# Four row loads may leave on ScalarE's queue, and the written-out order of a fused retention and mixer kernel is replaced

## The chip, the core and the metric

The kernel runs on one core of a Trainium2 chip. A core has five engines with instruction streams of their own: PE (TensorE, matrix products), DVE (VectorE), ACT (ScalarE), POOL (GpSimd) and SP (SyncE, which here only issues transfers). [...] Transfers are started from three places: SP's queue, ACT's queue (both "hardware" queues) and POOL's ("software"), and all are carried by the same 16 DMA engines. The metric is the device time of one execution in microseconds; lower is better.

## The reference: what is computed

A retention recurrence (eight heads, a fixed decay for each) over 768 steps is followed by an MLP mixer, for four batches:

```python
state = gamma[None, :, None, None] * state + np.einsum('bhd,bhe->bhde', k[:, :, t], v[:, :, t])
y[:, :, t] = scale * np.einsum('bhd,bhde->bhe', q[:, :, t], state)
...
x = np.ascontiguousarray(attn_out.transpose(0, 2, 1, 3)).reshape(B, S, H * D)
...
h = np.maximum(xt @ w_tok1, 0.0) @ w_tok2
u = x + h.transpose(0, 2, 1)
h2 = np.maximum(u @ w_ch1, 0.0) @ w_ch2
return (u + h2).astype(np.float32)
```

q, k and v are [4, 8, 768, 64]; the output is [4, 768, 512]; everything outside the chip is 32-bit.

## The kernel before

**Tiles.** 768 steps are six chunks of 128. The work of a batch falls into a *front* and a *back*. A front is done for each of four pairs of heads: k and q are scaled by powers of the decay (lines 343 and 345, tiles k16 and q16), turned so that the head dimension lies on partitions (kT, qT), multiplied into scores (453), masked on DVE (463, tile am) and multiplied with v (474). What comes from earlier chunks goes through the running state U (408 to 420), is scaled into block-diagonal tiles (434, 436) and multiplied with qT (483). The sum is cast to x16 (489), goes through the token mixer (503 with weights wt1, relu at 512 or 514, 523 with weights wt2), and is cast to u16 (529), copied to X (539) and turned into uT. A back takes uT of all four pairs through the channel mixer: the widening product (606 in batches 0 and 1; a seven-product scheme at 679 in batches 2 and 3), relu, and the narrowing product in the same seven-product manner (784, 810, 820, 830, 837), whose sums are added into X and written out (862, 746 to 761 for the last rows).

**Turning.** It is done in one of three ways, by a table: on PE with a copy behind it (377, 379, 568), or, in batches 2 and 3 throughout and for most uT of batch 1, by a transposing DMA on SP's queue (367, 553).

**Loads.** Rows of batches 0 and 1 and all weights come through POOL's queue (lines 257, 292, 295), which casts to 16 bit on the way. The first k comes on SP's. Rows of batches 2 and 3 (the table PLAIN) are loaded as they are, 384 KB each, by SP's queue at line 282; engines cast them afterwards (343, 345; v at 358 and 360). All of them share four buffers called row.

**Order.** The function builds a list of operations. Each has one way or several (which engine may do it, with a planner's cost in ns), operations that it needs, and buffers that it takes. No planner runs when the kernel is built: the string PLAN names each operation in the order of the program, the digit of its way where there is more than one, and the PSUM bank where it takes one. "+" and a digit puts that many *fillers* there, products of a zero tile at line 935 whose result nobody reads. placed() reads the string and the operations are emitted in that order, each to its engine's stream. An engine does its own instructions strictly in that order.

## Time and profile before

| | |
|---|---|
| three runs | 188.79, 189.35, 189.88 us; median 189.35 |
| the profiled execution | 189.72 us, of which 187.9 us are the profile's span |
| busy share of the span | PE 97%, DVE 87%, ACT 67%, POOL 19% |
| fillers | 62 products, 14.8 us busy |
| granted TensorE clock | 0.999 |
| chain that ended last | PE 82%, DMA 5%, ACT 5%, DVE 4% |

In rows of the timeline the columns are start, duration (both in us), engine, line, operation, tiles, and a count; the bracket holds the idle time before and what ended it. "SPq", "ACTq" and "POOLq" are the sequencers that issue transfers. In windows each row is a stretch, with the busy time of every engine in it, the granted clock, the mean share of the DMA engines and GB/s. In the groups the two numbers behind the bar are the total busy us and the mean ns of one instruction.

### The profile page before, as it was taken

What the parts mean: (1) busy time and instruction counts of PE and PEld (TensorE: products, weight loads), DVE (VectorE), ACT (ScalarE), POOL (GpSimd) and SP (SyncE); (2) the same over time, 40 slices, a digit from 0 to 9 for tenths busy, and PEclk for the clock granted to TensorE, in tenths of its full rate; (3) what the DMA queues carried; (4) which work ended last, traced back from release to release, by engine and by line L of the source; (5) the groups of instructions that cost most, each with busy time, mean ns of one, the idle gap of its engine ahead of it and who ended that gap; (6) DMA issues with size and microseconds to landing.
All of it is one profiled execution on the core that took longest, in us unless ns stands there. A gap on an engine that the chain in (4) does not pass through costs nothing.

```text
span 187.9 us, 5270 instructions
## 1 busy us (share of the span) xinstructions
PE 182.2 (97%) x2102; PEld 137.5 (73%) x2102; DVE 163.0 (87%) x424; ACT 126.2 (67%) x288; POOL 36.2 (19%) x45
## 2 busy tenths in 40 slices
PE   7999999999999999999999999999999999999993
PEld 3556789667679879767677988875589986656882
DVE  3789899978799998989896999999999988879973
ACT  7227789677868697579868696899975535682220
POOL 8992659520020001000103100210000000000000
PEclk9999999999999999999999999999999999999999
DMA  6999999999999799999999999998206464500133
GB/s 101 168 165 196 175 178 187 172 187 207 187 211 221 153 116 222 193 203 205 194 244 161 220 149 221 349 161 214 42 0 108 147 65 176 197 0 5 56 140 140
DMA packets 94233, 30.23 MB, mean 161 GB/s; under 512 B 84352, under 2 KB 91264, under 8 KB 94208
## 3 DMA queue, kind: packets, MB, share of 16 engines
q1 hardware_dynamic: 62560, 18.95, 56.1%
q0 software_dynamic: 30208, 8.46, 44.0%
q10 hardware_dynamic: 1440, 2.49, 4.5%
q8 instruction: 16, 0.26, 0.6%
q14 instruction: 9, 0.07, 0.2%
HBM read 26.74 MB, written 6.29 MB: 176 GB/s over the span
## 4 chain that ended last, share of the span: by engine, by line
PE 82%; DMA 5%; ACT 5%; DVE 4%; issue 1%; DVEq 0%; ACTq 0%
PE bank L606 14%; PE bank L820 13%; PE bank L679 12%; PE bank L830 9%; PE bank L935 6%; PE bank L523 6%; PE bank L503 6%; PE bank L453 3%; PE bank L474 3%; DMA qT<-q 3%; PE bank L746 3%; DMA uT<-u 2%; PE bank L483 2%; PE bank L408 2%; PE bank L377 2%; ACT h L622 2%
## 5 line engine op out<-in xcount | busy, mean ns | idle before, releaser
L463 DVE TENSOR_TENSOR am<-bank,mask 128x384 f16<-128x384 f32 x64 | 33.6, 549 | 4.4 <-PE bank L453 4.0
L606 PE MATMUL bank<-uT,wc 128*128 128x384 f16 x192 | 36.0, 326 | 0.0
L622 ACT ACTIVATE h<-bank 128x384 f16<-128x384 f32 x48 | 21.6, 491 | 9.1 <-PE bank L606 7.2
L606 PEld LDWEIGHTS <-wc 128*128 128x128 f16 x192 | 17.4, 98 | 9.1 <-DVE uT L575 0.2
L360 POOL CAST v<-row 128x768 f16<-128x768 f32 x7 | 7.4, 1067 | 76.6 <-DMA row<-in_v_dram 50.4
L696 DVE TENSOR_TENSOR h<-bank,us 128x384 f16<-128x384 f32 x36 | 18.9, 552 | 2.8 <-PE bank L679 1.8
L810 ACT COPY us<-bank 128x256 f32<-128x256 f32 x27 | 10.1, 377 | 15.8 <-PE bank L820 15.6
L820 PEld LDWEIGHTS <-hs 128*128 128x128 f16 x198 | 18.7, 98 | 2.4
L837 DVE TENSOR_TENSOR X<-X,bank 128x256 f32<-128x256 f32 x44 | 17.7, 414 | 2.4 <-PE bank L830 1.5
L691 ACT COPY us<-bank 128x384 f32<-128x384 f32 x36 | 16.3, 490 | 4.3 <-PE bank L679 3.3
L489 ACT CAST x<-bank 128x384 f16<-128x384 f32 x30 | 14.0, 487 | 6.7 <-PE bank L483 6.6
L420 DVE SCALAR_TENSOR_TENSOR U<-U,gp,bank 128x64 f32<-128x64 f32 x64 | 17.4, 275 | 1.0
L820 PE MATMUL bank<-wsum,hs 128*128 128x256 f16 x132 | 17.6, 273 | 0.0
L935 PE MATMUL bank<-zero 128*128 128x384 f16 x62 | 14.8, 382 | 1.1 <-DVE zero L928 1.1
L679 PE MATMUL bank<-hs,wsum 128*128 128x384 f16 x72 | 15.0, 326 | 0.1
L529 ACT CAST u<-bank 128x384 f16<-128x384 f32 x27 | 12.6, 487 | 3.5 <-PE bank L523 3.3
L523 PE MATMUL bank<-h,wt 128*128 128x128 f16 x192 | 14.8, 219 | 0.0
L434 ACT ACTIVATE diag<-U,gp 64x320 f16<-64x320 f32 x25 | 13.8, 558 | 0.4
L679 PEld LDWEIGHTS <-wsum 128*128 128x128 f16 x96 | 9.3, 97 | 6.4 <-issue 0.5
L503 PE MATMUL bank<-x,wt 128*128 128x128 f16 x192 | 13.7, 219 | 0.0
L830 PEld LDWEIGHTS <-h 128*128 128x128 f16 x132 | 12.5, 98 | 1.5
L539 ACT COPY X<-bank 128x384 f32<-128x384 f32 x28 | 13.4, 494 | 0.1
(89 smaller groups left out, 365.8 us busy)
## 6 DMA issues: line engine op xcount, KB each, us to landing
out_dram<-X SPq DMA_DIRECT2D x14, 256.0 KB, 4.3
row<-in_v_dram SPq DMA_DIRECT2D x8, 384.0 KB, 5.5
row<-in_k_dram SPq DMA_DIRECT2D x8, 384.0 KB, 6.0
row<-in_q_dram SPq DMA_DIRECT2D x8, 384.0 KB, 5.5
wc<-in_moe_w_ch_dram POOLq DMA_DIRECT2D x5, 512.0 KB, 12.6
out_dram<-X ACTq DMA_DIRECT2D x9, 256.0 KB, 3.0
row<-in_q_dram POOLq DMA_DIRECT2D x8, 192.0 KB, 6.1
v<-in_v_dram POOLq DMA_DIRECT2D x8, 192.0 KB, 8.4
```

Source lines behind the costliest of these rows:

```text
L420: nc.vector.scalar_tensor_tensor(out=u[:, c], in0=u[:, c - 1], scalar=gp[:, p:p + 1], in1=st, op0=ALU.mult, op1=ALU.add)
L463: nc.vector.tensor_tensor(am, SC[g].tile[:, :m * P].rearrange("p (i t) -> p i t", t=P), mask.to_broadcast([P, m, P]), ALU.mult)
L503: nc.tensor.matmul(acc[:, jt * P:(jt + 1) * P], wt1[:, i, jt * P:(jt + 1) * P], X16.tile[:, i], start=(i + jt == 0), stop=(i == NC - 1), s ...
L523: nc.tensor.matmul(Y[hf].tile[:, i * P:(i + 1) * P], wt2[:, jt, t], H1.tile[:, jt], start=False, stop=(jt == NJ - 1), skip_group_check=True)
L606: nc.tensor.matmul(acc[:, :SH], wc1[:, ct, ft * P:(ft + 1) * P], UT.tile[:, ct, sh * SH:(sh + 1) * SH], start=(ct == 0), stop=(ct == NP - 1))
L622: nc.scalar.activation(H2.tile[:, ft], A.tile[:, :SH], AF.Relu)
L679: nc.tensor.matmul(acc[:, :SH], left(ct), r[:, ct], start=first and ct == 0, stop=ct == 1, skip_group_check=True)
L696: nc.vector.tensor_tensor(into(hf)[:, ft], bank.tile[:, :SH], kept(j), ALU.add)
L820: nc.tensor.matmul(acc_[:, lo], l[:, j], r[:, j], start=first and j == 0, stop=j == K2 - 1, skip_group_check=True)
L830: nc.tensor.matmul(acc_[:, lo], l[:, j], r[:, j], start=first and j == 0, stop=j == K2 - 1, skip_group_check=True)
L837: (nc.vector if e == "DVE" else nc.gpsimd).tensor_tensor(dst(), dst(), b_(), ALU.add)
L935: nc.tensor.matmul(spare[:, :384], zero[:, :P], zero, start=True, stop=True)
```

## The change

Three things are edited. A plain row load has two ways now, SP's queue or ACT's. The load of k into the second half of a q tile no longer names the load of that q as a dependency in the planner's list. And PLAN is another string. The third decides everything about the order; the other two only say what the string may choose from.

```diff
 PLAN = (
-    "0b04000a0903010d05020c060f1h11i107+h1j00e1W11k0081X0h+41l01m0g+81w011v230k1z+21n41A2x50i1y1o1p0j1S01T11q1r0m"
...
+    "04000b050901030f0d0a060e021h1081i107+i1j01n11l21o1p1q1m1k11r1W31S01T1+81w021A1z1U41v560c2x20h1s1t01u00g1x+11Y1"
...
+        def emit_plain(e):
+            t = tile_of(s, [P, 2, NC, D], FP)
+            (nc.sync if e == "SP" else nc.scalar).dma_start(out=t, in_=src.rearrange("h (c p) d -> p h c d", p=P))
+
         def emit():
-            if plain:
-                t = tile_of(s, [P, 2, NC, D], FP)
-                nc.sync.dma_start(out=t, in_=src.rearrange("h (c p) d -> p h c d", p=P))
-                return
...
-            o = Op(ops, (-20, 0, b, p), [("SP", 500, 500, emit)], [], [s], dma=dma, behind=rows[-1] if rows else None)
+            o = Op(ops, (-20, 0, b, p), either(emit_plain, SP=(500, 500), ACT=(450, 450)) if plain else
+                   [("SP", 500, 500, emit)], [], [s], dma=dma, behind=rows[-1] if rows else None)
...
-            o = Op(ops, (-20, 0, b, p), [("POOL", 1000, 1000, emit)], [loads[b, p, "q"][2]], [], [s], dma=dma,
+            o = Op(ops, (-20, 0, b, p), [("POOL", 1000, 1000, emit)], [], [], [s], dma=dma,
```

Line numbers behind the edit are one higher in the changed kernel (935 becomes 936).

The new string holds 34 fillers where the old one held 62: 18 ahead of the first real product (17 before), and 16 between the real products of the first batch (45 before). 4 of the 24 plain row loads go by ACT's queue. Of the eight casts of a plain v to 16 bit five stand on POOL, two on DVE and one on ACT; before it was seven on POOL and one on ACT.

The first place is the head of POOL's stream, where the loads of batch 0 are issued. v, row and wt1, wt2 are the tiles that they fill. Before:

```order
L295 DMA v_122<-in_v_dram 128x12x64
L295 DMA row_90<-in_k_dram 128x12x64
L295 DMA v_179<-in_v_dram 128x12x64
L295 DMA row_116<-in_k_dram 128x12x64
L292 DMA row_225<-in_q_dram 128x2x384
L295 DMA v_257<-in_v_dram 128x12x64
L257 DMA wt1_78<-in_moe_w_tok1_dram 128x6x256
L257 DMA wt2_79<-in_moe_w_tok2_dram 128x2x768
```

Three loads of q stand ahead of these rows. In the changed kernel the whole head of the stream is:

```order
L295 DMA v_110<-in_v_dram 128x12x64
L292 DMA row_112<-in_q_dram 128x2x384
L292 DMA row_114<-in_q_dram 128x2x384
L295 DMA row_114<-in_k_dram 128x12x64
L292 DMA row_245<-in_q_dram 128x2x384
L295 DMA v_260<-in_v_dram 128x12x64
L295 DMA row_245<-in_k_dram 128x12x64
L292 DMA row_289<-in_q_dram 128x2x384
L295 DMA row_289<-in_k_dram 128x12x64
L295 DMA v_329<-in_v_dram 128x12x64
L257 DMA wt1_78<-in_moe_w_tok1_dram 128x6x256
L257 DMA wt2_79<-in_moe_w_tok2_dram 128x2x768
```

The first v has moved to the front, and one more load, the k of the last pair, now stands ahead of the two weights: ten loads in place of nine.

The second place is SP's stream where the turned tiles of batch 2's first pair are made: kT and qT are what its scores read, uT there is batch 1's. Before:

```order
L282 DMA row_1275<-in_k_dram 128x12x64
L367 DMA_TRANSPOSE kT_1375<-k16_1347 128x6x128
L282 DMA row_1411<-in_q_dram 128x12x64
L553 DMA_TRANSPOSE uT_1126<-u16_1314 128x6x128
L367 DMA_TRANSPOSE qT_1449<-q16_1373 128x6x128
L282 DMA row_1471<-in_v_dram 128x12x64
L282 DMA row_1515<-in_v_dram 128x12x64
L553 DMA_TRANSPOSE uT_1126<-u16_1446 128x6x128
```

In the changed kernel:

```order
L281 DMA row_1240<-in_k_dram 128x12x64
L554 DMA_TRANSPOSE uT_1254<-u16_1078 128x6x128
L281 DMA row_1333<-in_q_dram 128x12x64
L368 DMA_TRANSPOSE kT_1343<-k16_1322 128x6x128
L281 DMA row_1430<-in_v_dram 128x12x64
L368 DMA_TRANSPOSE qT_1487<-q16_1345 128x6x128
L281 DMA row_1510<-in_q_dram 128x12x64
L554 DMA_TRANSPOSE uT_1254<-u16_1268 128x6x128
L554 DMA_TRANSPOSE uT_1254<-u16_1404 128x6x128
```

The uT that stood between kT and qT now stands behind qT, and a load of v stands in its place.

The third place is ACT's stream a little earlier, where three of the four loads have come. h2 is the relu of batch 0's widening product, x16, k16, h1 belong to fronts of batches 1 and 2:

```order
L623 ACTIVATE h2_825<-bank6_1125 128x384
L281 DMA row_1159<-in_v_dram 128x12x64
L623 ACTIVATE h2_876<-bank4_1054 128x384
L490 CAST x16_1174<-bank7_1128 128x384
L623 ACTIVATE h2_825<-bank1_1162 128x384
L490 CAST x16_1174<-bank2_1151 128x384
L281 DMA row_1184<-in_k_dram 128x12x64
L344 ACTIVATE k16_1186<-row_901,gk_69 128x6x64
L513 ACTIVATE h1_1215<-bank1_1191 128x256
L623 ACTIVATE h2_876<-bank4_1181 128x384
L281 DMA row_1238<-in_q_dram 128x12x64
L623 ACTIVATE h2_876<-bank6_1217 128x384
```

Three or four other instructions stand between one load and the next; before, no load stood in ACT's stream at all.

More of the change, by code (lines that the diff above doesn't have):

```diff
@@ new lines @@
+    "7915n6h6ecj26l17a05P05QcK6f6B5Tce46i6cx6C16j5R05U06mck5W5cncI1c35S07c06k05X16n0cMcC6D1cf0J06o56pcN6A11dco0S0"
+    "7d0cQ46Edq7cR6q06rd25drcZ25V0cS7f46F36G0P06s06Hdsd06t0d86d16I6J6K6L01a7g1e7h7i7j7k1f6M1d577bdz0d9cT2da6udAdO3"
+    "6v0dPd3d66w1dQdBd7d4dh47I07K2dicU6N70367l16O6Q6R6Pdb10R0cVdcdC2dn7dd7m0dDdodEdpdj7J17e6x6V66W6S06T7n21356U16X0"
+    "7p0W07P4dk77qcL7Qdldmde1dfdgcW37R7r6Y77M18S06Z0V0dw17N0dF50U0cX7L1g7ocp700dGdHcYdx7OdR2dU71c7S7TbUdS71721e00T0"
+    "74dL37UdV8T0dy8m0e2dX1dYdt4e65dW750dTdM7V18n1760e10X0eb6dudZdNe7e3731cgec7X35127Ze477Ydv7v48i1dI0dJ0Y0cP17W0"
@@ L70 @@
+    "j0iw5iOixiyiziPicj16iA0iBiQj3j54jY5iCj2iDiJifiIiSiR6iGj4iTj6iXj7ke7iUiViEiHkfjbiYjcj8j9jejdhk0k62jZk7k0iFiejC"
+    "f31k1iWjajDk2jfjG4jEiKjgjijk6jH0jFjLk3jI3jN0jl0jM0jJk4k50jOjhjr1jPjRjQ0hG1jsjpjSjq0jTjUjvjKjVjW0jtjm4ju0jjjwjy"
+    "k8jxk9kajnjX1kbkgjA1jokhjzkijB1kckd0kjkkkl0"
 )
```

48 lines of the change are left out of this document (20 added, 28 removed).

## The prediction

> **What bounds the kernel now.** I read the page's totals first, then the busy time by stretches of 10 us, then the waits of PE.
>
> ```profile
> span 187.9 us, 5270 instructions
> PE 182.2 (97%) x2102; PEld 137.5 (73%) x2102; DVE 163.0 (87%) x424; ACT 126.2 (67%) x288; POOL 36.2 (19%) x45
> ...
> PE 82%; DMA 5%; ACT 5%; DVE 4%; issue 1%; DVEq 0%; ACTq 0%
> ...
> L935 PE MATMUL bank<-zero 128*128 128x384 f16 x62 | 14.8, 382 | 1.1 <-DVE zero L928 1.1
> ```
>
> PE is busy 97% of the span and carries 82% of the chain that ended last. But 62 of its products are fillers, so a busy PE is not yet a working PE. Where they stand decides.
>
> ```profile
> 1.13 5.62 PE L935 MATMUL bank<-zero 128*128 128x384 f16 x17 [1.13 <-DVE zero L928]
> ...
> 22.24 0.34 PE L935 MATMUL bank<-zero 128*128 128x384 f16 x1
> 22.42 0.83 PE L523 MATMUL bank<-h,wt 128*128 128x128 f16 x12
> ```
>
> All of them lie in the first 22.6 us (the first row and the last of them). Behind that PE hardly ever stops:
>
> ```profile
> PE bank L453 <- DMA qT<-q: 0.6, 1, 0.6
> PE bank L679 <- DMA uT<-u: 0.2, 1, 0.2
> PE bank L408 <- ACT h L622: 0.2, 1, 0.2
> ```
>
> So there are two regimes. Up to 22.4 us the first batch's data set the pace and fillers pass the time. From there on PE's own products do, with 1.0 us of named waits in 162 us. An order can win in the first regime what its data allow, and in the second about 1 us; it can lose more than that wherever it makes PE wait.
>
> **Fillers and the start.** The change takes 29 fillers out from between the real products and puts one more ahead of them. A late group of 9 in the chain of waits
>
> ```profile
> 15.12 1.57 PE bank L935 x9
> ```
>
> is 174 ns each, so 29 are worth 5.1 us if nothing stands behind them. I don't count on that, because something does: the token mixer's weights.
>
> ```profile
> 5.89 1.02 POOL L295 DMA_DIRECT2D v<-in_v_dram  x1
> 6.89 1.03 POOL L295 DMA_DIRECT2D row<-in_k_dram  x1
> ...
> 9.60 1.56 POOL L257 DMA_DIRECT2D wt<-in_moe_w_tok_dram  x2
> ```
>
> The issues by window give from issue to landing:
>
> ```profile
> v<-in_v_dram POOLq DMA_DIRECT2D x1, 192.0 KB, 6.9
> row<-in_k_dram POOLq DMA_DIRECT2D x1, 192.0 KB, 7.0
> wt<-in_moe_w_tok_dram POOLq DMA_DIRECT2D x1, 384.0 KB, 8.2
> wt<-in_moe_w_tok_dram POOLq DMA_DIRECT2D x1, 384.0 KB, 9.7
> ```
>
> The v of 5.89 lands at 12.8, the k of 6.89 at 13.9: this queue hands over a load of k every 1.1 us, and later loads lag more and more behind their issue. wt1, issued at 9.6, lands at 17.8 and wt2, issued at 10.4, at 20.1. In the new order one more k goes ahead of it, so wt2 lands at 21.2, and line 523 can't run earlier. Its relu comes to DVE behind a row of mask products; I take 21.6, against 22.42 now: 0.8 us. Two small corrections nearly cancel. The new order has one more turn of k and two more products of line 483 ahead of that point (6 and 2 products, 0.45 us at the 56 ns that 12 products of line 523 take each in 0.67 us), which is work won. Against it, it moves both x16 casts of the second pair from ACT to DVE, with a mask product between them:
>
> ```profile
> L489 DVE CAST x<-bank 128x384 f16<-128x384 f32 x2 | 1.1, 544 | 0.0
> L463 DVE TENSOR_TENSOR am<-bank,mask 128x384 f16<-128x384 f32 x64 | 33.6, 549 | 4.4 <-PE bank L453 4.0
> 23.09 0.83 PE L503 MATMUL bank<-x,wt 128*128 128x128 f16 x12
> ```
>
> Three of these are 1.6 us behind the relu, while PE has 12 products of line 523 and half of line 503 to do, 1.0 us: it waits 0.6. The term is **-0.7 us**. Its bounds: DVE works 22.0 of the 25 us from 7 to 32 us (the sum over five windows, below) and has much the same rows to do, so its 3.0 us of idle are all that any order can win here; and if the weights' delay of 1.1 us simply passes through, the start is 1.1 us slower.
>
> ```profile
> sum 25.00, PE 24.84 PEld 18.61 DVE 22.02 ACT 16.32 POOL 17.74; mean PE 4.97 PEld 3.72 DVE 4.40 ACT 3.26 POOL 3.55
> ```
>
> **Batch 2's first turned q.** PE's longest wait:
>
> ```profile
> 61.17 1.14 ACT L343 ACTIVATE q<-row,gy 128x384 f16<-128x384 f32 x2
> ...
> 63.23 1.96 SPq L553 DMA_TRANSPOSE uT<-u  x1
> 65.24 1.28 SPq L367 DMA_TRANSPOSE qT<-q  x1
> ...
> 70.65 0.51 PE L453 MATMUL bank<-qT,kT 64*128 64x128 f16 x12 [0.62 <-DMA qT<-q]
> ```
>
> q16 is ready at 62.3, but SP first waits for a uT and issues qT at 65.24. In the new order that uT stands behind qT, so qT can leave up to 2.9 us earlier, while the scores stand at nearly the same place among PE's products. The term is **-0.6 us**, all of the wait. The load of v that stands there now costs SP 0.44 us when its buffer is free (the row of 49.61 below), and the wait comes back only if SP sits there for over 2.3 us. What is late next is the uT itself, which now leaves later. Its reader, batch 1's widening product, starts over 10 us on:
>
> ```profile
> 77.86 3.41 PE L606 MATMUL bank<-uT,wc 128*128 128x384 f16 x20
> ```
>
> **The last uT.** Here PE waited for the transpose behind batch 3's last token mixer:
>
> ```profile
> 151.34 4.36 DMA uT<-u
> ...
> 151.95 0.82 PE L820 MATMUL bank<-wc,hs 128*128 128x256 f16 x6
> 152.60 0.82 PE L830 MATMUL bank<-wsum,h 128*128 128x256 f16 x6
> ...
> 155.74 0.65 PE L679 MATMUL bank<-uT,wc 128*128 128x384 f16 x3 [0.20 <-DMA uT<-u]
> ```
>
> A group of six narrowing products is 0.65 us from start to start, and a widening product 0.17 us (the 20 in 3.41 above). Between the last product of line 523 and the first that reads the last pair's uT stand six such groups and five widening products, 4.8 us; in the changed kernel six groups and nine, 5.4 us. That covers the wait: **-0.2 us**. If the transpose starts later by that much, nothing is won.
>
> **Loads on ACT, casts on DVE.** An unhindered load costs its sequencer 0.44 us, four of them 1.8 us on an engine that has idle time there (ACT 2.50 of 4 us). I take nothing for them on PE's path.
>
> ```profile
> 49.61 0.44 SPq L282 DMA_DIRECT2D row<-in_v_dram  x1
> 50.16 2.26 SPq L282 DMA_DIRECT2D row<-in_k_dram  x1
> 52.58 1.40 SPq L282 DMA_DIRECT2D row<-in_q_dram  x1
> ...
> 52.00:56.00 4.00, 4.00 (x40) 2.92 (x38) 3.92 (x8) 2.50 (x7) 0.76 (x1) 1.00 1.35 220
> ```
>
> The bound is a load close behind another: it held SP for 2.26 us, the third for 1.40. Nothing waited behind them on SP. On ACT casts and relus would, and PE for their banks. I stay near 0.44 since the new order leaves three or four instructions (1.5 to 2 us) between loads.
>
> [...]
>
> Two casts of v move from POOL, which is idle, to DVE. No row shows one on DVE; two scalings of f32 rows of half the size bound it (2 x 0.41 us).
>
> ```profile
> 60.39 0.41 DVE L345 TENSOR_SCALAR k<-row,gk 128x384 f16<-128x384 f32 x1
> 60.00:70.00 10.00, 10.00 (x126) 8.46 (x123) 9.67 (x30) 7.91 (x19) 0.00 (x0) 1.00 0.99 141
> 100.00:110.00 10.00, 10.00 (x130) 8.62 (x128) 8.19 (x21) 8.16 (x20) 2.54 (x2) 1.00 1.34 182
> ```
>
> That is 1.6 us of DVE. DVE has 1.8 us of idle around the later one and 0.3 around the earlier; without that cover PE pays up to 1.6. I take **+0.25**, near the covered end. The dropped dependency emits nothing. The last output still follows the last product by one add and one transfer, as now.
>
> **The sum.** -0.7 - 0.6 - 0.2 + 0.25 = -1.25 us. The profiled execution took 189.72 us (span 187.9 and 1.8 around it), so it would be 188.5; the median of the runs shown, 189.35, lies 0.37 below it, so I predict **188.1 us**, 0.7% less. With each term between its bounds the likeliest case reaches from 187.2 to 188.9.
>
> **Rivals.**
> 1. *The start wins more.* If DVE closes nearly all of its idle time, the start gives up to 3.0 us: 189.35 - 3.0 - 0.6 - 0.2 + 0.25 = 185.8, and with half of the further idle 187.0. For it: 29 fillers gone. Against: wt2 lands at 21.2 whatever PE does, and DVE is 88% full. (All 5.1 us would give 183.4; the weights exclude it.) 15%.
> 2. *Nothing is won.* The start pays the 1.1 us of the extra load and the two waits removed (0.8) come back elsewhere, as a new wait among 162 us in which every engine's stream was rearranged: 189.35 + 0 to + 0.9, about 189.4. For it: the old order left only 1.0 us of waits, so a new one is as likely to add as to remove. 27%.
> 3. *ACT stands behind its loads.* From the second load in a row held as SP was: 2.26 + 1.40 = 3.7 us, less ACT's 1.5 us of idle in that stretch, puts 2.2 us on the banks that PE waits for, and q16, scaled on ACT behind them, brings the 0.6 of the qT wait back: 188.1 + 2.2 + 0.6 = 190.9. It decides once a load holds ACT longer than its idle time there. Against: the loads are not back to back. 9%.
> 4. *The array goes cold.* The first 17 fillers took 331 ns each, later ones 174: early in this trace the array ran at half speed though the granted clock reads 1.00. If PE pauses long enough at the start, the products between 7 and 22.4 us (15.4 us less 44 fillers at 0.17 is 7.9, waits among them) take twice as long, some half of it under waits: up to +3 us, 191.1 on the forecast. The longest pause that I work out, ahead of wt1 (17.8 + 1.1 = 18.9), is about 2 us. 4%. [...]
>
> **Chances.** The forecast has 45%. About 0.5% (0.95 us) is what a measurement of this kernel can tell from no change. Below 188.4 lie rival 1 and four fifths of the forecast: 51%. Rival 2, the rest of the forecast and the mild end of rival 3 are within 0.5%: 36%. Above 190.3: 13%. The range 186.5 to 190.2 leaves out the far ends of rivals 1, 3 and 4; the likeliest case alone is 187.2 to 188.9.
>
> **What would show it.** The start: the first product of line 524 (formerly 523) at 21 to 22 us, with PE waiting in place of fillers, for the weights or DVE's casts; a start below 20.5 says rival 1, above 22.4 rival 2. The qT wait: no row of line 454 waiting for a qT transfer over 0.2 us. The end: no wait of line 680 for uT. ACT: its loads at 0.3 to 0.6 us each; 2 us or more says rival 3. The array: products of 128 columns at 56 ns from 8 us on; 107 ns would say rival 4. The forecast is wrong if PE's idle time behind 24 us passes 2 us.

## The result, and the profile after

| | before | changed |
|---|---|---|
| median of four runs each | 189.18 us (188.79 to 189.88) | 191.54 us (191.23 to 191.57) |
| the profiled execution | 189.72 us, span 187.9 | 191.23 us, span 189.4 |

The ratio is 1.0102 with a 95% interval of 1.0068 to 1.0135: the changed kernel is 1.0% slower. The forecast was 188.1 us, faster, with a range up to 190.2. It was wrong in its sign. Medians in this document are over all runs, while ratios leave out the few disturbed ones, the longest of which (264.81 us) is one of the twelve of "before, qT ahead of uT" below.

The totals of the changed kernel's profile, with the shares of the chain that ended last by engine:

```profile
span 189.4 us, 5219 instructions
PE 179.2 (95%) x2074; PEld 134.6 (71%) x2074; DVE 166.2 (88%) x430; ACT 123.9 (65%) x284; POOL 33.1 (17%) x43
...
PE 65%; DVE 16%; DMA 11%; ACT 4%; issue 1%; ACTq 0%; DVEq 0%
```

PE carried 82% of that chain and carries 65% now; DVE went from 4% to 16%, transfers from 5% to 11%. The chain itself (start, duration, what) names the two longest of its transfers:

```profile
38.24 14.71 DMA row<-in_k_dram
...
121.54 5.95 DMA out_dram<-X
```

The waits of PE in the changed kernel (total us, times, longest):

```profile
PE bank L380 <- DVE k L346: 1.7, 2, 1.5
PE bank L409 <- DVE X L540: 1.5, 1, 1.5
...
PE bank L475 <- DVE am L464: 0.5, 1, 0.5
PE bank L821 <- DVE X L838: 0.3, 1, 0.3
```

No wait for a qT and none for a uT is left, as predicted. But four others have come, and each has its place in the windows. In the changed kernel:

```profile
50.00:60.00 10.00, 9.22 (x112) 7.32 (x111) 7.77 (x13) 7.87 (x21) 0.82 (x1) 1.00 1.36 209
60.00:70.00 10.00, 9.57 (x115) 7.97 (x114) 9.86 (x29) 6.88 (x17) 0.00 (x0) 1.00 1.32 197
...
120.00:130.00 10.00, 8.38 (x115) 6.37 (x113) 8.28 (x23) 7.18 (x18) 1.66 (x2) 1.00 1.07 215
```

and before, where the stretch from 60 to 70 us stands in the prediction:

```profile
50.00:60.00 10.00, 10.00 (x116) 8.01 (x113) 9.79 (x19) 7.70 (x19) 1.48 (x1) 1.00 1.48 207
...
120.00:130.00 10.00, 10.00 (x127) 7.08 (x124) 9.45 (x26) 8.80 (x23) 1.72 (x2) 1.00 1.25 246
```

The first number behind the comma is PE's busy time. It was 10.00 of 10 us in all three stretches, and is 9.22, 9.57 and 8.38: 2.83 us idle. Since a busy PE may still run behind, I also compared when PE had got through the same amount of real work (its products other than fillers, each at its usual distance to the next), in the two profiled executions, counted from each one's first instruction:

| stretch of the changed kernel | gained (-) or lost (+), us |
|---|---|
| start, to 50 us | -1.0 |
| 53 to 58 us | +1.4 |
| 58 to 69 us | +0.7 |
| 69 to 79 us (the qT wait was here) | -0.8 |
| around 127 us | +1.4 |
| from there to 160 us (the uT wait was here) | -0.4 |
| the rest, the tail among it | +0.2 |
| sum | +1.5 |

The sum is the difference of the spans, 189.4 - 187.9. So the change won 2.2 us where I had looked, and lost 3.5 us at three places that I had put at nothing. Since the two orders differ, a place is good to some tenths only: with other choices of the usual distance the start comes out at -0.7, the place at 53 us at +1.0 and the one at 127 us at +1.9.

**At 53 us: a row lands late, and two engines stand for it in order.** The timeline of the changed kernel:

```profile
38.24 0.44 ACTq L281 DMA_DIRECT2D row<-in_k_dram  x1
...
50.41 0.39 ACTq L281 DMA_DIRECT2D row<-in_v_dram  x1
...
51.85 0.37 ACTq L281 DMA_DIRECT2D row<-in_k_dram  x1
...
52.98 0.61 ACT L344 ACTIVATE k<-row,gk 128x384 f16<-128x384 f32 x1 [0.48 <-DMA row<-in_k_dram]
52.98 0.42 DVE L346 TENSOR_SCALAR k<-row,gk 128x384 f16<-128x384 f32 x1 [2.17 <-DMA row<-in_k_dram]
...
53.52 2.07 ACTq L281 DMA_DIRECT2D row<-in_q_dram  x1
...
53.92 0.35 PE L475 MATMUL bank<-v,am 128*128 128x64 f16 x6 [0.53 <-DVE am L464]
```

The load of k that ACT issued at 38.24 landed at 52.95. DVE had reached its scaling 2.17 us before that and stood; behind the scaling in DVE's order stand the mask product that PE reads at 53.92, the kT copy and the sums hs. ACT's own scaling of the other half stood 0.48 us. Three issues were as cheap as I had taken them (0.44, 0.39, 0.37). The fourth took 2.07 us, until 55.59; the relu behind it started at 55.88, when the product that it reads was done, so no row shows that it cost anything.

**At 127 us: two transfers late together.**

```profile
116.90 2.27 SPq L863 DMA_DIRECT2D out_dram<-X  x1
...
119.63 1.48 SPq L281 DMA_DIRECT2D row<-in_v_dram  x2
...
121.54 0.34 ACTq L863 DMA_DIRECT2D out_dram<-X  x1
...
127.15 0.83 POOL L361 CAST v<-row 128x768 f16<-128x768 f32 x1 [1.79 <-DMA row<-in_v_dram]
...
127.52 0.86 ACT L540 COPY X<-bank 128x384 f32<-128x384 f32 x2 [0.26 <-DMA out_dram<-X]
127.52 0.56 DVE L540 COPY X<-bank 128x384 f32<-128x384 f32 x1 [1.62 <-DMA out_dram<-X]
...
128.22 0.51 PE L409 MATMUL bank<-v,k 128*64 128x64 f16 x20 [1.48 <-DVE X L540]
```

There are three buffers for X, so batch 3's first copy to X (line 540) overwrites batch 0's X and has to wait until its last rows have left. In the new order that last output stands in ACT's stream at 121.54, behind 768 KB of v that SP has just asked for, and takes 5.95 us. DVE stands 1.62 us for it, and PE for a bank that this copy empties. Before, those outputs were issued by 119.2 us and the copy at 124.34 did not wait. The same rows show a second thing that is late: the v itself, cast on POOL at 127.15.

**At 66 us** PE waits 0.3 us for a sum on DVE, which is busy 9.86 of 10 us there. I ran nothing on this place; the 0.7 us are read from the trace alone.

**The start** gained about what it should in this trace, but it has a flaw that I had not seen. The head of the changed kernel:

```profile
3.52 2.50 ACT L224 ACTIVATE gq<-us,lnsc,lnh 128x384 f32<-128x384 f32 x4
...
5.93 0.19 ACT L204 ACTIVATE gk<-lgs 128x8 f32<-128x8 f32 x1
...
6.16 0.82 DVE L346 TENSOR_SCALAR k<-us,gk 128x384 f16<-128x384 f32 x1 [3.47 <-ACT gk L204]
...
8.26 0.51 PE L380 MATMUL bank<-ident,k 128*128 128x128 f16 x6 [1.52 <-DVE k L346]
...
22.15 0.83 PE L524 MATMUL bank<-h,wt 128*128 128x128 f16 x12
```

ACT now makes the four gq ahead of gk, and the scaling of the first k needs gk. Before, gk came first, and the same first product ran 1.7 us earlier:

```profile
4.42 0.84 DVE L345 TENSOR_SCALAR k<-us,gk 128x384 f16<-128x384 f32 x2 [1.39 <-DMA us<-in_k_dram]
...
6.54 0.59 PE L379 MATMUL bank<-ident,k 128*128 128x128 f16 x6
```

The 1.0 us is a comparison of two executions, and the start differs between executions of one order by nearly as much. In the trace of "before, qT ahead of uT" run again, whose start is that of the kernel before, the first product runs at 6.22 and PE is 0.5 us ahead at 15 us: the first 17 fillers, slow at first, ended at 6.38 us there and at 6.75 here. In the trace of "batch 0's last output earlier", whose order is the changed kernel's up to 112 us, PE is 0.8 us behind the changed kernel's trace at 40 us. That trace then loses 0.5 us less at 53 us, because the row lands at nearly the same time, 53.30 in place of 52.95: part of what a start wins is handed back where PE waits for a row.

### The profile page after: what moved, and what is told of

It is laid out like the page before. It is cut to its first block, busy times and chain, and to the rows that moved or that the text cites. A ratio compares the mean times of both kernels' runs of the same rounds, so it can differ in the third digit from the quotient of the medians.

```text
span 189.4 us, 5219 instructions
## 1 busy us (share of the span) xinstructions
PE 179.2 (95%) x2074; PEld 134.6 (71%) x2074; DVE 166.2 (88%) x430; ACT 123.9 (65%) x284; POOL 33.1 (17%) x43
## 4 chain that ended last, share of the span: by engine, by line
PE 65%; DVE 16%; DMA 11%; ACT 4%; issue 1%; ACTq 0%; DVEq 0%
PE bank L821 13%; PE bank L680 13%; PE bank L831 11%; PE bank L607 8%; DMA row<-in_k_dram 8%; PE bank L504 4%; PE bank L524 4%; DMA out_dram<-X 3%; DVE U L421 3%; PE bank L747 3%; PE bank L454 3%; PE bank L475 2%; DVE hs L785 2%; DVE wsum L905 2%; DVE qT L388 2%; PE bank L484 2%
## 5 line engine op out<-in xcount | busy, mean ns | idle before, releaser
L623 ACT ACTIVATE h<-bank 128x384 f16<-128x384 f32 x48 | 22.2, 497 | 12.3 <-PE bank L607 12.1
L811 ACT COPY us<-bank 128x256 f32<-128x256 f32 x29 | 10.6, 374 | 20.3 <-PE bank L821 19.3
L361 POOL CAST v<-row 128x768 f16<-128x768 f32 x5 | 4.4, 873 | 85.1 <-ACT us L692 22.8
L435 ACT ACTIVATE diag<-U,gp 64x320 f16<-64x320 f32 x26 | 14.4, 559 | 3.7 <-DVE U L421 3.3
L530 ACT CAST u<-bank 128x384 f16<-128x384 f32 x29 | 13.3, 486 | 2.1 <-PE bank L524 2.0
L524 PE MATMUL bank<-h,wt 128*128 128x128 f16 x192 | 14.3, 219 | 0.0
L490 ACT CAST x<-bank 128x384 f16<-128x384 f32 x27 | 12.4, 486 | 2.6 <-PE bank L484 2.2
L524 PEld LDWEIGHTS <-wt 128*128 128x128 f16 x192 | 12.1, 98 | 1.4
L838 DVE TENSOR_TENSOR X<-X,us 128x512 f32<-128x512 f32 (+1 forms) x22 | 11.9, 554 | 1.1 <-ACT us L811 0.7
```

The costliest lines, as they stand in the source:

```text
L524: nc.tensor.matmul(Y[hf].tile[:, i * P:(i + 1) * P], wt2[:, jt, t], H1.tile[:, jt], start=False, stop=(jt == NJ - 1), skip_group_check=True)
L623: nc.scalar.activation(H2.tile[:, ft], A.tile[:, :SH], AF.Relu)
L838: (nc.vector if e == "DVE" else nc.gpsimd).tensor_tensor(dst(), dst(), b_(), ALU.add)
```

## The experiments

All ratios are to the kernel before, run beside it on the same chip; the interval is 95%. No kernel here leaves out work whose result is read. "C" is the changed kernel.

| edit | median us | ratio |
|---|---|---|
| C: two scalings of k later | 190.65 | 1.0067 (1.0042 to 1.0091) |
| C: batch 0's last output earlier | 191.38 | 1.0101 (1.0078 to 1.0125) |
| C: both | 190.17 | 1.0044 (1.0024 to 1.0065) |
| C: all plain loads on SP | 194.31 | 1.0257 (1.0222 to 1.0293) |
| C: gk ahead of gq | 195.95 | 1.0328 (1.0280 to 1.0375) |
| the same, first ACT load later | 192.31 | 1.0148 (1.0109 to 1.0187) |
| the same, first ACT load earlier | 191.13 | 1.0071 (1.0041 to 1.0102) |
| C: both, and v loads ahead of an output | 191.26 | 1.0072 (1.0046 to 1.0098) |
| C: these three, and gk ahead of gq | 195.57 | 1.0293 (1.0248 to 1.0339) |
| C: both, and 32 fillers ahead | 190.60 | 1.0049 (1.0022 to 1.0076) |
| C: both, 26 fillers ahead, two outputs early on ACT | 190.88 | 1.0058 (1.0034 to 1.0082) |
| before, without its 45 inner fillers | 190.71 | 1.0047 (1.0024 to 1.0070) |
| before's order, four plain loads on ACT | 196.50 | 1.0332 (1.0272 to 1.0393) |
| before, qT ahead of uT | 190.23 | 1.0026 (0.9993 to 1.0060) |
| the same again | 189.64 | 1.0026 (0.9998 to 1.0054) |
| the same, and a cover for the last uT | 189.73 | 0.9999 (0.9968 to 1.0029) |

### Scaling k later

The two scalings that stand for the late row are moved behind what else is ready on their engines; no transfer is touched. Rows of DVE's and ACT's streams:

```diff
 L464 TENSOR_TENSOR am<-bank,mask 128x384
-L346 TENSOR_SCALAR k<-row,gk 128x6x64
 L464 TENSOR_TENSOR am<-bank,mask 128x384
...
 L785 TENSOR_TENSOR hs<-h,hs 128x768
+L346 TENSOR_SCALAR k<-row,gk 128x6x64
 L905 TENSOR_TENSOR wsum<-wc 128x1536
...
 L281 DMA row<-in_k_dram 128x12x64
-L344 ACTIVATE k<-row,gk 128x6x64
 L513 ACTIVATE h<-bank 128x256
+L344 ACTIVATE k<-row,gk 128x6x64
```

> The changed kernel with one edit: the two scalings of batch 2's second k (one on DVE, one on ACT), which wait for a row that lands at 52.9 us, stand behind the work that they hold up: on DVE behind a mask product, a copy of kT and three sums, on ACT behind a relu. Theory A (the early row blocks DVE and ACT, and PE's 0.53 and 0.26 us of waits at 54 us come from it): those two waits go, PE reaches the same amount of work 0.8 to 1.3 us earlier at 58 us, and 190.2 to 190.8 us against 191.5. Rival B (DVE is full in this stretch, so that a wait only moves): PE waits elsewhere by 65 us, and under 0.4 us is won, 191.1 to 191.6.

190.65 us, 0.9 less than the changed kernel's 191.54 (0.7 less by the two ratios). In the timeline DVE's scaling has no idle time before it any more:

```profile
54.43 0.41 DVE L346 TENSOR_SCALAR k<-row,gk 128x384 f16<-128x384 f32 x1
```

PE's waits of 0.5 and 0.3 us at line 475 are gone, and by the count of real work PE gets through this stretch 1.1 us quicker. So the loss at 53 us is the place of these two instructions in two in-order streams, given when the row lands. (The two kernels were timed beside different runs of the one before; their two intervals, 1.0042 to 1.0091 and 1.0068 to 1.0135, overlap. The traces are what tells them apart.)

### Batch 0's last output earlier

```diff
-L863 DMA out_dram<-X 128x512
+L863 DMA out_dram<-X 128x512 x2
 L811 COPY us<-bank 128x256
...
 L692 COPY us<-bank 128x384
-L863 DMA out_dram<-X 128x512
 L490 CAST x<-bank 128x384
```

> The changed kernel with one edit: the last output of batch 0 stands on ACT's queue right behind the output before it (about 115.5 us) and not at 121.5 us. Its data are finished long before. Theory A (batch 3's first copy to X waits for the landing of this output at 127.4 us, and through it PE waits 1.48 us at 126.7): the wait goes, PE has 1.0 to 1.5 us less to make up, 190.0 to 190.5 us. Rival B (the loads and kT and qT transposes, issued late behind SP's outputs, would hold PE by as much anyway): under 0.4 us, 191.1 to 191.6.

191.38 us, nothing that can be told from the changed kernel. The wait for X is gone and a wait of the same size stands in its place:

```profile
PE bank L409 <- POOL v L361: 1.5, 1, 1.5
```

Here the rival was right: the v was as late as the output, and the first of two late transfers hides the second. The wait table of the changed kernel named only the one that came last. (Its rows bear this out: POOL's cast of v ended at 127.98 and DVE's copy to X at 128.08.)

### Both

> Both edits together. Theory A: the gains add, 2.0 to 2.8 us, 188.7 to 189.5 us, as fast as the kernel before or a little faster. Rival B: 190.7 or more.

190.17 us, less than either edit but more than the 188.7 to 189.5 expected. The wait for v stays. And something new shows in the windows of its first microseconds:

```profile
8.00:10.00 2.00, 1.74 (x30) 1.55 (x32) 1.05 (x11) 0.00 (x0) 2.00 (x3) 0.50 1.76 154
10.00:12.00 2.00, 2.00 (x23) 1.23 (x18) 1.96 (x6) 0.61 (x1) 2.00 (x4) 0.66 2.21 156
```

The third number from the right is the granted clock: 0.50 and 0.66. The first products after the fillers, in this kernel,

```profile
8.26 0.82 PE L380 MATMUL bank<-ident,k 128*128 128x128 f16 x6 [2.38 <-DVE k L346]
```

and in the one with the later scalings alone:

```profile
8.26 0.51 PE L380 MATMUL bank<-ident,k 128*128 128x128 f16 x6 [2.47 <-DVE k L346]
```

The head of the program is the same in both. After a pause of 2.38 us the six products took 0.82 us, after one of 2.47 us they took 0.51. By the count of real work the first kernel has lost 1.0 us to the changed kernel at 20 us. Of its twelve runs eight have a mean clock of 0.996 or more and lie from 189.52 to 190.51 us; four have 0.991 and lie from 190.67 to 190.94. So a pause at this place brings half speed in some executions and not in others, and costs about 1 us here where it does. (Not in every order: with the last output alone earlier, four of six runs have a clock of 0.989 to 0.991 and take 190.93 to 191.74 us, the other two 191.45 and 191.71.) The pause is there because of gk behind gq.

The length of the pause does not decide. In all traces here but one the stretches at one clock last whole multiples of 3.41 us; in this one full speed from 4.51 to 7.93 us, half speed from 7.93 to 11.34. Counted in such steps, and leaving out the end of the program, the clock fell behind seven steps, in which PE was busy for 0.57 to 1.47 us (1.36 here), and behind no step with 1.70 or more. It came back behind steps with 3.08 us or more and not behind those with 2.56 or less. The kernel with the later scalings is the one exception: PE was busy 1.45 us in its step from 4.34 to 7.75, and the clock held. So it matters how much of a step PE fills, and where the steps lie, which differs from run to run (4.51 to 7.93 us here, 4.34 to 7.75 there). A step need not be idle for the fall: 1.47 us of work in one were too little.

### All plain loads on SP

```diff
 L295 DMA us<-in_k_dram 128x12x64
+L281 DMA row<-in_k_dram 128x12x64
+L281 DMA row<-in_v_dram 128x12x64
+L281 DMA row<-in_k_dram 128x12x64
+L281 DMA row<-in_q_dram 128x12x64
 L281 DMA row<-in_k_dram 128x12x64
```

The same four rows leave ACT's stream.

> The changed kernel with its four plain loads of ACT put on SP's queue, at the same places of the written-out order. In the changed kernel the first of them took 14.7 us from issue to landing, while weights came on POOL's queue. Theory A (the weights share the DMA engines with it, whatever queue it is on): on SP it takes 12 to 16 us too and lands at 51 to 54 us; 191.0 to 192.0 us. Rival C (ACT's queue is the slow one): it lands within 7 us, as SP's loads did in the kernel before, DVE's wait of 2.2 us at 53 us is gone, and about 190.3 us.

194.31 us, 2.6% slower than before, worse than either side expected. SP has nothing to wait for, so it asked for the rows as early as their buffers were free, while POOL's queue still carried batch 1's rows and the weights:

```profile
28.30 0.38 SPq L281 DMA_DIRECT2D row<-in_k_dram  x1
31.68 0.39 SPq L281 DMA_DIRECT2D row<-in_v_dram  x1
```

```profile
PE bank L409 <- DMA v<-in_v_dram: 2.8, 1, 2.8
```

The four loads took 10.5, 10.9, 14.6 and 17.8 us to land, against 14.7 of the first one on ACT's queue: beside POOL's traffic none of them came near the medians of 4.0 to 4.7 us that SP's loads have in the changed kernel. But it matters when it is issued. Batch 1's own v, issued by POOL at 41.2, now took 22.1 us (17.1 in the changed kernel, issued at 37.5), and PE waited 2.8 us for it; behind that wait the granted clock was 0.50 for 3.41 us. So ACT's stream served the changed kernel as a brake: its in-order place held the first load back until 38.24.

Why 14.7 us for 384 KB, when SP's loads in the changed kernel have medians of 4.0 to 4.7? Its first packet came at 42.2, 4.0 us after the issue; what it waited for no row shows. The queues between 43 and 52 us in the changed kernel (packets, MB, share of the engines' time):

```profile
q0 software_dynamic: 1587, 1.38, 93.5%
q10 hardware_dynamic: 1389, 0.35, 29.6%
```

q0 is POOL's, q10 ACT's. They move nearly as many packets, 1587 and 1389, but POOL's are 870 bytes on average and the load's 252. So the load got 0.35 of 1.73 MB, 39 KB per us. With all plain loads on SP the counts of POOL's queue and SP's are 1232 and 1232 from 36 to 39 us, and 924 and 926 from 50 to 56 us; in other stretches they differ (1763 and 949 from 39 to 42 us). How packets of two queues come to be served in these shares no row shows.

### gk ahead of gq

```diff
-L224 ACTIVATE gq<-us,lnsc,lnh 128x384 x4
 L204 ACTIVATE gk<-lgs 128x8
 L205 ACTIVATE gy<-lgs,lnsc 128x8
+L224 ACTIVATE gq<-us,lnsc,lnh 128x384 x4
```

> The changed kernel with one edit: the two small exponentials gk and gy (0.19 and 0.28 us on ACT) stand ahead of the four of gq (2.5 us), as in the kernel before. In the changed kernel DVE waits 3.5 us for gk, and the first real product starts at 8.26 us instead of 6.54. Theory H (the late head is part of the loss: the first pair of heads starts later and PE idles 1.5 to 2.8 us there, in one run long enough that the array dropped to half speed): the first product starts by 6.7 us, no run's array is cold at 8 us, and 5 us of work are done 0.3 to 1.2 us earlier; 190.3 to 191.2 us against 191.5, with less spread. Rival W (loads and weights set the start, so the head has slack): under 0.3 us, 191.2 to 191.7.

195.95 us, 3.3% slower than before. The first product runs at 7.04 in place of 8.26, but by 20 us the same work is done as in the changed kernel: transfers and DVE pace that stretch, as the rival said. What costs the time is elsewhere. ACT's and PE's rows:

```profile
39.18 5.56 ACTq L281 DMA_DIRECT2D row<-in_k_dram  x1
44.79 0.49 ACT L623 ACTIVATE h<-bank 128x384 f16<-128x384 f32 x1 [5.35 <-issue]
...
46.73 4.00 PE L607 MATMUL bank<-uT,wc 128*128 128x384 f16 x12 [0.28 <-ACT h L623]
```

and, behind that, the window with its granted clock:

```profile
47.00:50.00 3.00, 3.00 (x11) 1.44 (x10) 1.91 (x8) 0.05 (x1) 0.00 (x0) 0.50 1.26 192
```

Issuing the first load held ACT for 5.56 us (0.44 in the changed kernel), PE waited 3.6 us for ACT, and behind that pause the clock was 0.50: twelve widening products took 4.00 us where 20 had taken 3.41. With the head edited by two instructions the load stands 0.9 us later than in the changed kernel, and its issue blocks. The time alone does not do it: with both edits above it was issued at 39.31, in 0.44 us.

Two kernels move that load in the same head. Four instructions later:

```diff
-L281 DMA row<-in_k_dram 128x12x64
 L623 ACTIVATE h<-bank 128x384
 L344 ACTIVATE k<-row,gk 128x6x64
 L623 ACTIVATE h<-bank 128x384
 L623 ACTIVATE h<-bank 128x384
+L281 DMA row<-in_k_dram 128x12x64
```

> e5_head (195.95 us) with the first plain load of ACT four instructions later. In e5_head this load held ACT for 5.56 us (0.44 in the changed kernel), and a fetch of ACT's instructions (8 KB on the instruction queue) lies inside that time, at 43.1 us; in the changed kernel and in e1 to e3 the fetch came 1.3 to 1.6 us ahead of the load. Theory I (the load and the fetch meet, and ACT stands until the fetch is through; a row or two of shift decide it): the hold is under 1 us, and 191 us or less. Rival (the load itself is held while weights fill the DMA engines, wherever it stands): ACT is held 4 us or more again, and 194.5 us or more.

and two earlier:

```diff
+L281 DMA row<-in_k_dram 128x12x64
 L623 ACTIVATE h<-bank 128x384
 L623 ACTIVATE h<-bank 128x384
-L281 DMA row<-in_k_dram 128x12x64
```

> e5_head with the first plain load of ACT two instructions earlier (e10 had it four later, and the hold of 5.56 us was gone). Theory I (a meeting of the load with a fetch of instructions): the fetch on the instruction queue moves out of the load's issue, the hold is under 1 us, and 190 to 192 us. Rival (once the load leaves before about 40 us it is held, since too much is queued ahead of it on the engines; it is let go when some of that is through): ACT is held 4 us or more, and 194 to 197 us.

In both the hold is gone: the load is issued at 42.26 in 0.44 us, and at 38.24 in 0.43 us. The times are 192.31 and 191.13 us; in the first the row lands at 54.06, 1.1 us later than in the changed kernel. The second is no worse than the changed kernel; so the 5.56 us are what made 195.95, but gk ahead of gq by itself wins at most a few tenths. The rival, that a load which leaves before 40 us is held, is refuted by the one at 38.24. The theory of a fetch of instructions had the holds right: a fetch of 8 KB on an instruction queue (q14 in the profile) lies inside the two holds of a single load, at 43.11 here and at 42.51 in the kernel further down that joins this head to three edits (held from 39.11 to 44.14), and outside the issue in the two kernels with the load moved, at 37.41 and 42.75. But the hold of 4.80 us in the next section has no such fetch in it, and nothing here shows that the fetch is the cause; it stays open.

### Loads on ACT in the old order

before's order with the first four plain loads (v, k, q, k of batch 2) issued by ACT at the places where the old list has them, some of them close behind each other:

```diff
 L540 COPY X<-bank 128x3x128
 L435 ACTIVATE diag<-U,gp 64x5x64
+L281 DMA row<-in_v_dram 128x12x64
+L281 DMA row<-in_k_dram 128x12x64
 L623 ACTIVATE h<-bank 128x384
 L623 ACTIVATE h<-bank 128x384
+L281 DMA row<-in_q_dram 128x12x64
 L623 ACTIVATE h<-bank 128x384
+L281 DMA row<-in_k_dram 128x12x64
```

> The order of the kernel before, with its first four plain loads (v, k, q, k) on ACT's queue at the places where SP had them: the move of loads by itself. On SP the second and third held the sequencer 2.26 and 1.40 us. Theory L (ACT is held as SP was, and the loads go out as soon as their buffers are free): one of the loads holds ACT 2 us or more, PE waits for ACT, and 0.7 to 4 us slower than before (190.1 to 193.5). Rival (an issue costs ACT 0.4 us, which its idle time covers): within 0.4 us of the kernel before.

196.50 us, 3.3% slower, and beyond what the expectation allowed.

```profile
50.35 4.80 ACTq L281 DMA_DIRECT2D row<-in_q_dram  x1
```

```profile
PE bank L504 <- ACT h L623: 4.9, 1, 4.9
```

The four took 0.44, 2.06, 4.80 and 1.69 us; on SP nothing stood behind such holds, on ACT a relu did, and PE behind the relu. Behind PE's wait the granted clock was 0.50 for 6.83 us. This is the prediction's third rival at more than its price.

### The v loads ahead of an output, and three edits at once

On top of both edits, SP asks for the two rows of v ahead of batch 0's output:

```diff
 L281 DMA row<-in_k_dram 128x12x64 x2
+L281 DMA row<-in_v_dram 128x12x64 x2
 L863 DMA out_dram<-X 128x512
-L281 DMA row<-in_v_dram 128x12x64 x2
```

> The two edits of e3_both, and one more: on SP's queue the two loads of v for batch 3's last pairs stand ahead of an output of batch 0 (256 KB) and not behind it. In e3_both the wait for X was gone, and PE waited 1.37 us at the same product for POOL's cast of the second v, whose row landed at 127.0 us. Theory A2 (two things were late at that place, and the second is the place of the v loads behind the output): the rows land 1 to 2.5 us earlier, the wait falls under 0.4 us, and 188.9 to 189.4 us. Rival (the DMA engines are full there, and the rows land as late as before): 189.9 to 190.3.

191.26 us: the wait for v is gone, and the wait for X back at 1.4 us, since now that output is the later one. Then with gk ahead of gq as well:

> e6_v_first with the head of e5_head. If the gains add: 188.0 to 188.9 us, clearly faster than the changed kernel and at or below the kernel before (189.4). If the head has slack: as e6_v_first.

195.57 us; the hold is there again (5.03 us, at 39.11) and PE waits 3.0 us for ACT's scaling of k. It says nothing new on the v.

### What the fillers are worth

The kernel before, with every filler between the real products taken out (45 of 62). A piece of the string, where "+4" and "+8" are fillers:

```diff
-0081X0h+41l01m0g+81w011v230
+0081X0h1l01m0g1w011v230
```

> The kernel before without its 45 fillers between the real products (the 17 ahead of them stay). Theory F (a filler only passes time in which PE would wait; the first batch is paced by its loads and by DVE): within 0.4 us of the kernel before. Rival G (fillers stand in the way of real products): 0.5 to 2 us faster. Rival K (without them the array idles and drops to half speed): the 128-column products of the first 20 us take 107 instead of 56 ns, and 0.5 to 3 us slower.

190.71 us, 0.5% slower. This kernel's stretch from 12 to 24 us,

```profile
12.00:24.00 12.00, 10.00 (x129) 8.46 (x130) 9.21 (x25) 7.08 (x15) 6.11 (x7) 0.50 1.80 183
```

and that of the kernel before:

```profile
12.00:24.00 12.00, 11.84 (x182) 8.49 (x181) 10.86 (x31) 7.65 (x17) 6.14 (x7) 1.00 1.80 183
```

The granted clock is 0.50 in place of 1.00 in the whole stretch. By the count of real work this trace is 1.0 us ahead at 10 us (its first 17 fillers ended at 5.58 and not at 6.75, and the first product ran at 5.41) and 1.5 us behind at 25 us: it lost 2.4 us there at half speed. It cost no more because data pace much of the stretch; the whole kernel is 1.2 us slower by the medians and 0.9 by the ratio. So the inner fillers, which I had taken to pass time, kept the clock up.

So I put fillers into the pause ahead of the first product of the kernel with both edits, 32 in place of 18 ("w" in place of "i" in the string):

```diff
-i107+i1j01n11l21o1p1q1m
+i107+w1j01n11l21o1p1q1m
```

> e3_both with 32 fillers ahead of the first real product where the changed kernel has 18. In the changed kernel the fillers are used up 1.5 to 2.5 us before the first real product (8.26 us), and in some runs of e3_both (mean granted clock 0.991) the array then ran at half speed to about 11.5 us: those took 190.5 to 190.9 us, and those with a clock of 0.997 and more 189.5 to 190.2. Theory K (the gap lets the array go cold in some runs, for about 1 us): no run has a mean clock under 0.996, 189.5 to 189.9 us. Rival (the extra fillers themselves hold the first product, 14 of them at 0.16 to 0.32 us are 2.3 to 4.5 us against a gap of 2.4): the first product starts later than 8.6 us, and 190.3 us or more.

190.60 us, no better. The clock was 0.996 or more in all twelve runs. But the fillers last till 9.1 us, and the first product stands behind them:

```profile
9.08 0.50 PE L380 MATMUL bank<-ident,k 128*128 128x128 f16 x6
```

0.8 us later than the data allowed. The clock's gain was spent on fillers.

Last, 26 fillers there, and one more output of batch 0 moved from SP to ACT ahead of the others, so that the v can leave earlier:

```diff
-L863 DMA out_dram<-X 128x512      (SP)
+L863 DMA out_dram<-X 128x512      (ACT)
```

> e3_both with two edits: 26 fillers instead of 18 ahead of the first real product (they should end close to 8.3 us, where that product starts; 32 ended at 9.1 and held it up), and the output of batch 0 that stood on SP ahead of the two loads of v goes to ACT's queue ahead of the three outputs there. Theory A3 (the gap at the head, the blocked DVE, X and v are what the new order lost): the array stays warm, PE waits under 0.5 us at 128 us, and 188.3 to 189.2 us, at or below the kernel before. Rival (the outputs on ACT's queue and v's rows share the engines, and the wait only changes its name once more): 189.5 us or more.

190.88 us, no better either. The wait for v fell from 1.4 to 0.9 us, and new ones came ahead of it:

```profile
117.90 4.82 SPq L281 DMA_DIRECT2D row<-in_v_dram  x2
...
119.01 0.56 DVE L648 TENSOR_TENSOR hs<-uT 128x768 f16<-128x768 f16 x1 [1.44 <-DMA uT<-u]
```

By the count of real work it loses 1.5 us from 117 to 122 us.

### The qT wait by itself

The second term of the prediction, alone, in the kernel before: on SP the turned q leaves ahead of batch 1's uT.

```diff
 L282 DMA row<-in_q_dram 128x12x64
+L367 DMA_TRANSPOSE qT<-q 128x6x128
 L553 DMA_TRANSPOSE uT<-u 128x6x128
-L367 DMA_TRANSPOSE qT<-q 128x6x128
```

> The kernel before with one edit: on SP the first qT of batch 2 stands ahead of the uT that it stood behind. The prediction's term by itself: PE's wait of 0.62 us for that qT goes, 0.4 to 0.7 us faster than before. Rival (the wait moves on to the mask products behind the scores, DVE being busy 9.67 of 10 us there): the wait goes and under 0.25 us is won.

The same kernel was run a second time, for its trace:

> The same kernel as e12_before_qT, for a trace. Theory (something waits in the 0.62 us's place): PE's wait for qT at 70 us is gone in the trace, and another wait of 0.4 us or more has come up behind it. Rival (the wait is still there, because qT is held by something else than the uT ahead of it). In both, the times are as in e12, within 0.4 us of the kernel before or a little slower.

1.0026 in both, with intervals that hold 1: no gain. The trace shows the 0.6 us wait gone and PE 0.8 us ahead until 150 us. Of these 0.5 were there at 15 us, where nothing differs but the execution; at the edit's own place PE goes from 0.3 to 1.0 us ahead. Then it waits for the last uT:

```profile
155.62 0.65 PE L679 MATMUL bank<-uT,wc 128*128 128x384 f16 x3 [0.84 <-DMA uT<-u]
```

In the kernel before this product ran at 155.74 behind a wait of 0.20: the same moment. PE came there earlier and waited longer; the transposed tile came when it came. So the last piece covers that wait with a group of line 830, six products, put ahead of it:

```diff
+L830 MATMUL bank<-wsum,h 128x256 x6
 L679 MATMUL bank<-uT,wc 128x384 x4
-L830 MATMUL bank<-wsum,h 128x256 x6
```

> e14_before_qT_again (the kernel before with the first qT ahead of a uT) with one more edit: at 154 us a group of six narrowing products (line 830, 0.65 us), which does not need the last uT, stands ahead of the widening products that wait for it, and not behind. Theory (the 0.62 us won at 70 us are lost again at the last uT, whose landing does not move with PE): the wait of 0.84 us falls to about 0.2, and the kernel is 0.4 to 0.7 us faster than before: 188.9 to 189.2 us against 189.6. Rival (that uT was not what held the end; DVE is): the time stays within 0.25 us of the kernel before.

0.9999 (0.9968 to 1.0029). The uT wait is gone from the trace, but this execution (190.76 us, 1.0 above the median) has waits of 0.8, 0.4 and 0.4 us elsewhere. Two waits of 0.8 us in all can be taken out of the kernel before without any gain in its time that could be measured. For the qT alone the intervals leave room for a gain of 0.1 us at most; for both together for 0.6.

## Why the prediction was wrong, and where it was right

**Fillers and the start (-0.7): right in the trace, not confirmed as a gain.** PE was 1.0 us ahead by 50 us, but executions of one order differ there by 0.5 to 0.8, and a lead is partly handed back at 53 us. The landing was right: wt2 came at 21.37, forecast 21.2. The sign that I had named was poor, though: line 524's first product came at 22.15 and not at 21 to 22, because other work stood ahead of it. And the step "data set the pace" held even where gk came 1.7 us late. (The side remark on all 5.1 us is a slip: 189.35 - 5.1 - 0.6 - 0.2 + 0.25 is 183.7, not 183.4.) What the removed fillers would cost, I had left to a rival of 4%. In the changed kernel nothing: its four runs have a granted clock of 1.0.

**The qT wait (-0.6) and the last uT (-0.2): right as events.** Both waits are gone, worth 0.8 and 0.4 us by place. As a gain in the time, the first is not confirmed: alone it won nothing. I named as "late next" the uT behind it on SP; it was the last uT, 85 us on.

**Casts of v on DVE (+0.25):** no wait of PE for a v from DVE shows. The v that PE waits for in the experiments is one on POOL, late because its row is.

**Loads on ACT (0): this step failed.** I priced what it costs to issue a load, 0.44 us, and that was right. I did not ask when the row lands and who stands for it. A row of the trace before would have told: the loads of POOL in the start lagged more and more, and I used that for wt2 alone. For the k of 38.24 the same reasoning, with weights in flight, gives a landing far behind the 5.5 to 6.0 us that SP's row loads have as medians in the kernel before; DVE's order had its scaling ahead of PE's mask product. It cost 1.4 us by place, and the experiment that moves the two scalings wins back 0.9 us in the medians, 0.7 by the ratios and 1.1 in the trace.

**Batch 0's outputs: no step at all.** The new string moves the last of them on ACT, behind v loads, and the fourth front needs its buffer. I had said that the last output of the program follows the last product as before, and looked at no other. The place cost 1.4 us, but moving the output alone wins nothing there: v is late at the same moment. No run removed both, so that the 1.4 us would come back is not shown.

**The sum: the failed step that decides the sign.** It entered the waits that the new order removes as gains, and new waits as 0, and left them to the second rival, which it held to at most 0.9 us. The reason given was that the old order left 1.0 us of waits. That bounds what an order can win; what a new order can lose has no bound there. Nor does the 0.9 hold by the rival's own terms: the start that pays 1.1 us is more by itself. The second rival's mechanism came true ("a new wait among 162 us in which every engine's stream was rearranged"), with 3.5 us in three places against 2.2 us won. At its right size it would have given 189.35 - 2.2 + 3.5 = 190.7, slower; with the difference of the profiled executions, +1.5, it is 190.9, and 191.5 was measured.

**Rivals 3 and 4** are real, though they are not what made the changed kernel slow. One of its four loads did take 2.07 us, the sign named for rival 3, but no wait came of it, and its clock stayed up (1.0). In three experiments a load held ACT for 4.8 to 5.6 us, and in seven the array went to half speed (mean granted clock 0.962 to 0.991 in their profiled executions). That a pause of about 2 us is too short for rival 4 no run shows: behind pauses of 2.0 us (both edits, and v loads ahead of an output) and 2.38 us (both edits) the clock was 0.50. The condition that the prediction gave for being wrong, PE idle for over 2 us behind 24 us, came true: 2.87 us (161.0 less the 158.13 that PE was busy from 24 to 185 us; it was 1.46 before).

**Open:** the 0.7 us at 58 to 69 us; why one ACT load holds for 5 us and its neighbour two instructions off does not; what the place at 127 us would give with both late transfers early; and why no combination of repairs, each right in the trace, brought the new order below the old one. The best of them, both edits, is still 0.4% slower than the kernel before; its eight runs with a clock of 0.996 or more have a median of 189.74, 0.4 us above the 189.38 run beside them.

## What to carry to other kernels

When a whole order is replaced, the waits of the old trace say what can be won, not what can be lost: go through each in-order stream of the new order for every instruction that needs a landing row or a buffer that an output still holds, and set its place against the landing time that such a transfer has in that stretch, with the traffic of that stretch (here 14.7 us, beside medians of 4.0 to 4.7). A wait that goes away, or a better start, wins nothing if a later point is paced by data, and of two transfers that are late together the trace names one. Fillers between real products may be what keeps the array at full speed (here 1.70 us of work in each 3.41 were enough); take them out only where the time is filled by something else.

## What the runs showed of the hardware that I had not expected

- A load in packets of 252 bytes beside weights in packets of 870 got nearly as many packets and so 0.35 of 1.73 MB: 14.7 us for 384 KB on ACT's queue, 10.5 to 17.8 on SP's.
- Issuing one load held ACT for 0.37 to 0.45 us in most places, 2.07 us for the last of four in the changed kernel (1.47 and 1.48 with the later scalings), 2.06, 4.80 and 1.69 us for the later three of four that stood close together, and 5.56 and 5.03 us for a single one, which fell to 0.43 and 0.44 when it was moved by two and by four instructions.
- A pause of PE of 2.38 us was followed by a granted clock of 0.50, one of 2.47 us at the same place was not. In all traces but one the clock changed only at steps of 3.41 us, falling behind steps in which PE was busy 0.57 to 1.47 us (with 1.45 it held once) and never behind one with 1.70 or more; half speed in the first batch cost 1.0 us where it lasted 3.41 us and 2.4 where it lasted 13.65.
